# The exponent test of a float64-to-float32 conversion on ScalarE instead of VectorE, and the last small expert slot's first layer one step earlier

## The chip, the core and the metric

One core of one Trainium2 chip runs the whole program as one launch. The metric is the device time in microseconds, the median over several executions. TensorE is called PE here, VectorE DVE, ScalarE ACT, GpSimd POOL, and SP is the engine whose queue issues most of the DMAs.

## What is computed

Three stages follow one another on activations of 4 x 544 x 512: attention with a window and 32 global tokens, a mixture of eight experts with sticky routing, and a gated feed-forward block with a short convolution. Cut to what matters:

```python
x = attention(q_l, k_l, v_l, q_g, k_g, v_g)          # (4, 544, 512)
# experts: a token keeps the expert of the one before it, or takes a fresh one
h = np.maximum(x[b, s] @ w1[e], 0.0)                  # w1: 8 x 512 x 1024
out[b, s] = p[e] * (h @ w2[e])                        # w2: 8 x 1024 x 512
# feed-forward block; w_in, conv_w and w_out come as float64
h = np.maximum(x @ w_in, 0.0)                         # 512 x 1024
gate = 1.0 / (1.0 + np.exp(-conv3(h, conv_w)))
y = (h * gate) @ w_out                                # 1024 x 512
```

## The kernel before

Attention and routing fill the first 174 us. The expert stage then runs 20 slots, numbered 2 to 21, of up to 128 tokens of one expert each. With these inputs an expert takes one to four slots, and where its first slot holds few tokens (32 or less) that slot is "small": it multiplies the raw float32 weights with 32 token columns (`few_l1`, L1394, and `few_l2`, L1410). The other slots use weights split into a high part `wh` (a cast on ACT, L1045) and a low part `wl` (a subtraction on DVE, L1046), three matmuls for each product (L1110 for the first layer, L1126 for the second). Slots 2, 9, 13, 16 and 21 are small.

`step(s)` writes one slot's program: first layer of slot s, fetch of later weights, gather and transposition of slot s+1 (`turn_x`), the split of the first layer's weights if slot s+1 changes the expert (`resplit(s+1, 1)`, under an `If` at L1331), second layer of slot s-1 with its scatter to `y_dram` (L1083, on POOL), transposition of the hidden values of slot s (`turn_h`), the split of the second layer's weights (`resplit(s, 2)`). Each engine runs its own instructions in the order in which this is written. Since an `If` may write `wl`, PE's first layer waits until DVE has come past that `If`, taken or not.

Beside it, 16 chunks of `w_in` and `w_out` are turned from float64 into float32, one in each of the steps 3 to 18 (`convert`, `conv64`). The raw chunk lies in `fx`, `hi` and `lo` being the two 32-bit halves of each number. Six DVE instructions (L1012 to L1017) put the sign, exponent and fraction together and test the exponent, POOL adds the rounding bit (L1018), and one more DVE instruction, kept as a function in `self.conv`, flips a bit and masks tiny numbers to zero. It is called in the next step, right behind `turn_x` (`while self.conv`), and appears as L1019. The conversion stands ahead of the second layer where the next slot keeps its expert, and at the step's end where it doesn't.

The last slot, 21, is written by `last`, and the step of slot 20 is an ordinary `step`. In `last`, ACT and DVE also split the converted `w_in` into the registers of the first layer's weights (`split`), ACT loads the table for the sigmoid (L1234), and `load0` (L1501, called at the end of step 20's second layer) reads the first 544 rows of `y_dram` back for the feed-forward block; `scale0` (L1509) and `xt0` (L1516 to L1519) scale and transpose them. Each scatter waits for the one before it to land, `load0` waits for the scatter of slot 19, the scatter of slot 20 waits for `load0`, and the block's own first loads (L1535) wait for the scatter of slot 21. The block's units (L1585 first layer, L1609 and L1602 on ACT, L1604 and L1620 on DVE) then run to the end with its second layer (L1662).

Of the kernel before, what the change touches and what calls it, by code (L numbers as in the profile page):

```python
# [17 lines left out]
P = 128  # L18
# [985 lines left out]
DVE_F = (1, 3, 5, 7)  # L1004
POOL_K = {1: (), 2: ()}


def conv64(nc, raw, out):
    hi, lo = raw[:, :, 1], raw[:, :, 0]
    v = nc.vector  # L1010
    a = out.bitcast(I32)
    v.tensor_scalar(a, hi, 3, 0x7FFFFFFF, ALU.logical_shift_left, ALU.bitwise_and)  # L1012
    v.scalar_tensor_tensor(a, hi, -2 ** 31, a, ALU.bitwise_and, ALU.bitwise_or)
    v.tensor_scalar(hi, hi, 1, 21, ALU.logical_shift_left, ALU.logical_shift_right)
    v.tensor_scalar(hi, hi, 897.0, -1.0, ALU.is_ge, ALU.mult)
    v.scalar_tensor_tensor(a, lo, 29, a, ALU.logical_shift_right, ALU.bitwise_or)
    v.tensor_scalar(lo, lo, 28, 1, ALU.logical_shift_right, ALU.bitwise_and)  # L1017
    nc.gpsimd.tensor_tensor(a, a, lo, ALU.add)  # L1018
    return lambda: v.scalar_tensor_tensor(a, a, 0x40000000, hi, ALU.bitwise_xor, ALU.bitwise_and)  # L1019

# [32 lines left out]
class Moe:  # L1053
    def __init__(self, sig, tc, W, ident, x_dram, y_dram, rt, w1, w2, wi, wo):
# [3 lines left out]
        self.sig = sig  # L1058
        self.xs, self.xt, self.ht, self.hs, self.next, self.chg, self.sm = {}, {}, {}, {}, {}, {}, {}
        self.conv, self.raw = [], {}  # L1060

# [125 lines left out]
    def run(self, cw6, cwr, cw, f2):  # L1187
        nc, W, tc = self.nc, self.W, self.tc
        n = NSLOT - 3
        self.f2 = f2  # L1190
        for s in range(NA, n - 1):
            self.step(s)
            if s == NA + 17:
                self.conv.append(conv64(nc, cw6, cwr))
        self.last(n - 1, cwr, cw)
# [12 lines left out]
    def last(self, s, cwr, cw):  # L1208
        nc, W, f2 = self.nc, self.W, self.f2
        x, xs, hp = self.xt.pop(s), self.xs.pop(s), self.h_tile()  # L1210
# [4 lines left out]
        def split(a, b):  # L1215
            for k in range(a, b):
                W.split_k(1, W.f, k, nc.gpsimd if k in POOL_K[1] else nc.vector)

        def resplit(a, b):
            with self.tc.If(self.chg[s] != 0):  # L1220
                for k in range(a, b):
                    W.split_k(2, W.s, k, nc.gpsimd if k in POOL_L else nc.vector)

        def few1():
            self.few_l1(xs, hp, hs)
            split(0, NKC)

# [4 lines left out]

        self.either(s, few1, full1)
        nc.scalar.activation(self.sig, self.sig, AF.Sigmoid)  # L1234
        self.layer2(s - 1)
        self.fetch(s - 1, 2)
        self.conv_w(cwr, cw)
        self.rt.late_flag(s + 1, self.px.tile([P, 4, P], F32, tag="tr", name="lf")[0:1, 0, 0:1])
        for i in range(5):
            f2.scale0(i, self.ps)  # L1240
        resplit(0, 4)
        for i in range(2):
            f2.xt0(i, self.px)
        t = [self.ps.tile([P, 4, P], F32, tag="tr", name="hlp") for _ in range(2)]
        yp = self.y_tile()

        def few2():
            self.few_turn(hs, t[0])
            self.few_l2(hs, yp, y)

# [192 lines left out]
    def step(self, s):  # L1443
# [6 lines left out]
        self.turn_x(s + 1)  # L1450
        while self.conv:
            self.conv.pop()()
        if s < NA + 16:
# [284 lines left out]
def moe_kernel(ctx, tc, q_l, k_l, v_l, q_g, k_g, v_g, w_gate, w_local, w1, w2, w_in, conv_w, w_out, out):  # L1738
    nc = tc.nc
    outf = out.rearrange("b s d -> (b s) d")  # L1740
    with tc.manual_schedule():
# [38 lines left out]
        def hook(n, end):  # L1780
# [119 lines left out]
```

## Time and profile before

| what | us |
|---|---|
| median of 3 runs (lowest, highest) | 621.88 (618.85, 623.83) |
| the profiled execution: its own time | 619.98 |
| span from its first to its last instruction | 618.2 |
| PE busy in the span | 571.3 |

Times in the rows further down count from the start of the span. A row of the timeline gives an instruction's (or a run of equal instructions') start, its length, engine, line, operation, output and inputs, count, and in brackets how long the engine stood idle just before and what ended that. Rows of the windows give the busy time of each engine in a stretch, then the granted TensorE clock as a share of 2.4 GHz, the share of DMA time and GB/s.

### The profile page before, as it was taken

The page shows a single profiled execution, that of the slowest core. Times are in us where ns is not written, and L with a number is a line of the kernel's source. Part 1 is how long each engine was busy: PE and PEld are TensorE (multiplying, and loading weights), DVE is VectorE, ACT ScalarE, POOL GpSimd, SP SyncE. Part 2 cuts the span into 40 slices and gives each one's busy share as a digit, 9 for nine tenths or more (in the row PEclk, how much of TensorE's full clock was granted, in tenths as well). Part 3 has the DMA queues.
Part 4 walks back from the last instruction along what each step waited for, and adds up shares of the span by engine and source line. Part 5 has one row for each costly group of instructions (what it writes and reads, how often), then busy time and mean ns, then how long its engine had stood idle before and what let it go on. Part 6 is the DMA issues. An engine that isn't in the chain of part 4 may idle for free. (4 is left out here: it accounts for less than half of the span.)

```text
span 618.2 us, 16382 instructions
## 1 busy us (share of the span) xinstructions
PE 571.3 (92%) x6108; PEld 477.8 (77%) x6108; DVE 407.5 (66%) x854; ACT 308.3 (50%) x623; POOL 173.7 (28%) x226
## 2 busy tenths in 40 slices
PE   7779899888889999989989799979899999999997
PEld 6567677666667888768767688769898998998986
DVE  7868576875974867885687885366864484383330
ACT  5755555565225544652454724547753564463441
POOL 7655830034022423143132431010302313300100
PEclk9998899999999999999999989979899999999999
DMA  9989949568229765576357593322110201000001
GB/s 230 216 184 247 237 114 209 175 216 255 83 64 323 285 228 218 160 282 236 135 177 264 187 319 107 125 83 64 52 36 25 77 18 35 35 0 35 36 35 51
DMA packets 60643, 90.57 MB, mean 147 GB/s; under 512 B 25726, under 2 KB 34198, under 8 KB 60504
## 3 DMA queue, kind: packets, MB, share of 16 engines
q1 hardware_dynamic: 57016, 78.93, 42.1%
q0 software_dynamic: 3520, 10.23, 4.9%
q8 instruction: 65, 1.06, 0.7%
q14 instruction: 42, 0.34, 0.2%
HBM read 125.87 MB, written 15.79 MB: 229 GB/s over the span
## 5 line engine op out<-in xcount | busy, mean ns | idle before, releaser
L1604 DVE SCALAR_TENSOR_TENSOR fc<-f_hp,cw,fc 128x544 f32<-128x544 f32 (+2 forms) x66 | 51.7, 783 | 73.3 <-ACT fc L1602 71.9
L1046 DVE TENSOR_TENSOR wl<-ws,wh 128x512 fp32r<-128x512 f32 (+1 forms) x80 | 64.6, 869 | 8.1 <-ACT wh L1045 6.9
L1045 ACT CAST wh<-ws 128x512 fp32r<-128x512 f32 (+1 forms) x84 | 58.0, 770 | 1.7 <-DMA ws<-in_moe_w_dram 0.7
L1126 PE MATMUL yp<-wh,gh 128*128 128x512 f32 x136 | 54.8, 403 | 0.9 <-ACTq L1331 0.9
L1662 PE MATMUL f<-wh,fh 128*128 128x512 f32 (+1 forms) x144 | 54.8, 381 | 0.0
L1126 PE MATMUL yp<-wl,gh 128*128 128x512 f32 x136 | 53.5, 394 | 1.1 <-DVEq L1331 0.7
L1662 PE MATMUL f<-wh,fl 128*128 128x512 f32 (+1 forms) x144 | 54.4, 378 | 0.0
L1662 PE MATMUL f<-wl,fh 128*128 128x512 f32 (+1 forms) x144 | 54.4, 378 | 0.0
L1126 PE MATMUL yp<-wh,gl 128*128 128x512 f32 x136 | 53.3, 392 | 0.0
L1110 PE MATMUL hp<-wl,xh 128*128 128x512 f32 x136 | 45.5, 407 | 8.4 <-DVEq L1331 5.3
L1083 POOL DMA_INDIRECT y_dram<-ys,sidx x22 | 25.4, 1156 | 86.5 <-ACT ys L1438 38.7
L1309 ACT ACTIVATE hs<-hp 128x512 f32<-128x512 f32 x34 | 18.7, 594 | 61.3 <-PE hp L1110 61.3
L278 ACT ACTIVATE pr<-sp,nm 128x128 f32<-128x128 f32 x128 | 36.6, 376 | 24.7 <-DVE nm L275 24.7
L1110 PE MATMUL hp<-wh,xh 128*128 128x512 f32 x136 | 46.2, 412 | 0.2 <-ACT ys L1413 0.2
L1071 POOL DMA_INDIRECT xs<-x_dram,gidx x22 | 26.9, 1223 | 65.3 <-DMA ws<-in_moe_w_dram 34.0
L1110 PE MATMUL hp<-wh,xl 128*128 128x512 f32 x136 | 44.7, 401 | 0.0
L1018 POOL TENSOR_TENSOR wf<-wf,fx 128x512 int32<-128x512 int32 x16 | 20.9, 1304 | 74.0 <-DVE fx L1017 65.6
L1110 PEld LDWEIGHTS hp<-wl,xh 128*128 128x128 f32 x136 | 25.8, 193 | 15.8 <-DVEq L1331 6.6
L1609 ACT ACTIVATE f_hp<-f 128x544 f32<-128x544 f32 x31 | 19.4, 625 | 37.4 <-PE f L1585 33.4
L1103 DVE TENSOR_TENSOR gl<-hlp,gh 128x512 fp32r<-128x512 f32 x34 | 22.0, 685 | 18.3 <-ACT gh L1425 13.9
L1438 ACT COPY ys<-yp 128x512 f32<-128x512 f32 x15 | 8.9, 591 | 50.0 <-PE yp L1126 47.2
L1671 ACT COPY fy<-f 128x512 f32<-128x512 f32 (+1 forms) x18 | 10.1, 564 | 46.7 <-PE f L1662 46.7
(381 smaller groups left out, 1529.0 us busy)
## 6 DMA issues: line engine op xcount, KB each, us to landing
ws<-in_moe_w_dram SPq DMA_DIRECT2D x42, 2048.0 KB
fx<-y_dram SPq DMA_DIRECT2D x17, 256.0 KB
raw<-in_k_l_dram SPq DMA_DIRECT2D x16, 256.0 KB
x_dram<-x SPq DMA_DIRECT2D x16, 256.0 KB
fx<-in_moe_w_in_dram SPq DMA_DIRECT2D x8, 512.0 KB
fx<-in_moe_w_out_dram SPq DMA_DIRECT2D x8, 512.0 KB
out_dram<-fy SPq DMA_DIRECT2D x16, 256.0 KB
VA<-in_v_l_dram SPq DMA_DIRECT2D x20, 192.0 KB
```

The source lines that it names most:

```text
L278: nc.scalar.activation(pr[:, hp, :], sp[:, hp, :], AF.Exp, bias=nm[:, hp:hp + 1], scale=-1.0)
L1018: nc.gpsimd.tensor_tensor(a, a, lo, ALU.add)
L1045: (cp.tensor_copy if cp else self.nc.scalar.copy)(h, src[n][:, k, :])
L1046: eng.tensor_tensor(l, src[n][:, k, :], h.bitcast(F32), ALU.subtract)
L1071: self.nc.gpsimd.indirect_dma_start(out=xs, out_offset=None, in_=self.x_dram[0:n, :], in_offset=bass.IndirectOffsetOnAxis(ap=self.rt.gidx[ ...
L1083: self.nc.gpsimd.indirect_dma_start(out=self.y_dram[:, :], out_offset=bass.IndirectOffsetOnAxis(ap=self.rt.sidx[:, s:s + 1], axis=0), in_= ...
L1103: self.nc.vector.tensor_tensor(hl[1][:, a:a + 4], t, hl[0][:, a:a + 4].bitcast(F32), ALU.subtract)
L1110: self.nc.tensor.matmul(hp[c], a[:, k, :], b[:, 512 * c:512 * c + 512], start=k == 0 and m == 0, stop=k == NKC - 1 and m == 2)
L1126: self.nc.tensor.matmul(yp, a[:, k, :], b, start=k == 0 and m == 0, stop=k == NFC - 1 and m == 2)
L1604: nc.vector.scalar_tensor_tensor(c[:, a:b], hp[:, a + t:b + t], self.cw[:, t, f:f + 1], c[:, a:b], ALU.mult, ALU.add)
L1609: self.nc.scalar.activation(hp[:, 1:S + 1].rearrange("p (a c) -> p a c", a=2), p[:, :, 0:272], AF.Relu)
L1662: self.nc.tensor.matmul(yp[:, cs], x[:, c], w[:, cs], start=f == 0 and n == 0, stop=f == NFC - 1 and n == 2)
```

## The change

The test of the exponent moves to ACT: `Abs` of the upper half, read as float32, into a buffer `m`, then `Sign` of a limit less that, written as an integer, which is -1 (all bits) or 1. DVE then masks with one `tensor_tensor` ahead of POOL's addition; the constants are chosen so that no bit has to be flipped. The deferred instruction and `self.conv` go. `m` is the fifth input buffer of the feed-forward block, one for all conversions; `lim` is a column that was padding. In `last`, which now also writes slot 20's step, the split of `w_in` and the sigmoid's table come ahead of slot 19's second layer, slot 21's small first layer comes ahead of `turn_h` of slot 20 and so ahead of its second layer, its transposition takes a buffer of its own, and its scatter comes ahead of the last three `xt0`. The diff, without the passing on of `lim` and its `memset`:

```diff
@@ conv64
+TINY = (9 - 2.0 ** -20) * 2.0 ** -18
-def conv64(nc, raw, out):
+def conv64(nc, raw, out, m, lim):
     hi, lo = raw[:, :, 1], raw[:, :, 0]
-    v = nc.vector
-    a = out.bitcast(I32)
-    v.tensor_scalar(a, hi, 3, 0x7FFFFFFF, ALU.logical_shift_left, ALU.bitwise_and)
-    v.scalar_tensor_tensor(a, hi, -2 ** 31, a, ALU.bitwise_and, ALU.bitwise_or)
-    v.tensor_scalar(hi, hi, 1, 21, ALU.logical_shift_left, ALU.logical_shift_right)
-    v.tensor_scalar(hi, hi, 897.0, -1.0, ALU.is_ge, ALU.mult)
+    v, a, n = nc.vector, out.bitcast(I32), m.shape[0]
+    nc.scalar.activation(m, hi.bitcast(F32), AF.Abs)
+    nc.scalar.activation(m.bitcast(I32), m, AF.Sign, bias=lim[0:n], scale=-1.0)
+    v.tensor_scalar(a, hi, 3, 0x3FFFFFFF, ALU.logical_shift_left, ALU.bitwise_and)
+    v.scalar_tensor_tensor(a, hi, -2 ** 30, a, ALU.bitwise_and, ALU.bitwise_or)
     v.scalar_tensor_tensor(a, lo, 29, a, ALU.logical_shift_right, ALU.bitwise_or)
     v.tensor_scalar(lo, lo, 28, 1, ALU.logical_shift_right, ALU.bitwise_and)
+    v.tensor_tensor(a, a, m.bitcast(I32), ALU.bitwise_and)
     nc.gpsimd.tensor_tensor(a, a, lo, ALU.add)
-    return lambda: v.scalar_tensor_tensor(a, a, 0x40000000, hi, ALU.bitwise_xor, ALU.bitwise_and)
...
@@ Moe.run
-        for s in range(NA, n - 1):
+        for s in range(NA, n - 2):
             self.step(s)
...
@@ Moe.last
-        nc, W, f2 = self.nc, self.W, self.f2
+        nc, W, f2, p = self.nc, self.W, self.f2, s - 1
+        self.small(s)
+        self.layer1(p)
+        self.fetch(p, 1)
+        self.turn_x(s)
+        self.resplit(s, 1)
...
-        def few1():
+        r = nc.values_load(self.rt.esi[0:1, 5, s:s + 1], min_val=0, max_val=1,
+                           engines=[mybir.EngineType.Activation, mybir.EngineType.DVE])
+        with self.tc.If(r != 0):
+            split(0, NKC)
+        nc.scalar.activation(self.sig, self.sig, AF.Sigmoid)
+        self.layer2(p - 1)
+        self.fetch(p - 1, 2)
+        f2.load0()
+        with self.tc.If(self.sm[s] != 0):
             self.few_l1(xs, hp, hs)
-            split(0, NKC)
+        self.turn_h(p)
+        self.resplit(p, 2)
...
-        self.either(s, few1, full1)
-        nc.scalar.activation(self.sig, self.sig, AF.Sigmoid)
-        self.layer2(s - 1)
-        self.fetch(s - 1, 2)
+        tq = self.px.tile([P, 4, P], F32, tag="tr", name="hlq")
+        self.either(s, lambda: self.few_turn(hs, tq), full1)
         self.conv_w(cwr, cw)
...
+        self.layer2(p)
+        self.fetch(p, 2)
...
-        self.either(s, few2, full2)
+        self.either(s, lambda: self.few_l2(hs, yp, y), full2)
         resplit(4, NFC)
...
+        self.scatter(s, y)
         for i in range(2, 5):
-            f2.xt0(i, self.px)
-        self.scatter(s, y)
+            f2.xt0(i, self.ps if i == 4 else self.px)
@@ Moe.step
-        while self.conv:
-            self.conv.pop()()
...
-        if s == hi - 2:
-            self.f2.load0()
```

On DVE, the conversion of one chunk (`wf` is the converted weight, `fx` the raw chunk). Before:

```order
L1012 TENSOR_SCALAR wf_3966<-fx 128x512
L1013 SCALAR_TENSOR_TENSOR wf_3966<-fx,wf_3966 128x512
L1014 TENSOR_SCALAR fx<-fx 128x512
L1015 TENSOR_SCALAR fx<-fx 128x512
L1016 SCALAR_TENSOR_TENSOR wf_3966<-fx,wf_3966 128x512
L1017 TENSOR_SCALAR fx<-fx 128x512
```

and now, where `fx` is also the mask:

```order
L1014 TENSOR_SCALAR wf_3967<-fx 128x512
L1015 SCALAR_TENSOR_TENSOR wf_3967<-fx,wf_3967 128x512
L1016 SCALAR_TENSOR_TENSOR wf_3967<-fx,wf_3967 128x512
L1017 TENSOR_SCALAR fx<-fx 128x512
L1018 TENSOR_TENSOR wf_3967<-wf_3967,fx 128x512
```

Two of the four fast single-input instructions are gone, and a `TENSOR_TENSOR` has come.

On DVE, the stretch from `turn_x` of the next slot (`xl`) to the `If` that PE's next first layer waits for. Before:

```order
L1340 COMPARE_AND_BRANCH
L1340 UNCONDITIONAL_BRANCH
L1103 TENSOR_TENSOR xl<-xlp,xh 128x512
L1340 UNCONDITIONAL_BRANCH
L1019 SCALAR_TENSOR_TENSOR wf_3966<-wf_3966,fx 128x512
L1324 TENSOR_LOAD esi
L1331 COMPARE_AND_BRANCH
```

and now:

```order
L1349 COMPARE_AND_BRANCH
L1349 UNCONDITIONAL_BRANCH
L1103 TENSOR_TENSOR xl<-xlp,xh 128x512
L1349 UNCONDITIONAL_BRANCH
L1333 TENSOR_LOAD esi
L1340 COMPARE_AND_BRANCH
```

The instruction L1019 that stood ahead of the flag's `TENSOR_LOAD` and the `If` (L1331, now L1340) is gone.

On ACT, the last slots: `ys_3454` is the output buffer of slot 20 in the build before, `wf_3966` the converted `w_in`. Before:

```order
L1045 CAST wh_2_2729<-wf_3966 128x1024
L1045 CAST wh_3_2731<-wf_3966 128x1024
L1340 UNCONDITIONAL_BRANCH
L1045 CAST wh_0_2725<-wf_3966 128x1024
L1045 CAST wh_1_2727<-wf_3966 128x1024
L1340 UNCONDITIONAL_BRANCH
L1234 ACT_TABLE_LOAD
L1234 ACTIVATE warm<-warm 128x1
L1340 COMPARE_AND_BRANCH
L1413 COPY ys_3454<-yp 32x128 x4
L1340 UNCONDITIONAL_BRANCH
L1438 COPY ys_3454<-yp 128x512
```

and now, where `ys_3456` is the buffer of slot 19:

```order
L1045 CAST wh_0_2726<-wf_3967 128x1024
L1045 CAST wh_1_2728<-wf_3967 128x1024
L1045 CAST wh_2_2730<-wf_3967 128x1024
L1045 CAST wh_3_2732<-wf_3967 128x1024
L1231 UNCONDITIONAL_BRANCH x2
L1233 ACT_TABLE_LOAD
L1233 ACTIVATE warm<-warm 128x1
L1349 COMPARE_AND_BRANCH
L1422 COPY ys_3456<-yp 32x128 x4
L1349 UNCONDITIONAL_BRANCH
L1447 COPY ys_3456<-yp 128x512
L1349 UNCONDITIONAL_BRANCH
```

The four casts and the table load stood behind slot 21's small first layer and ahead of slot 20's output; they now stand ahead of slot 19's.

## Rows read from the trace of the kernel before

**Rows 1.** Page, part 1, and one group of part 5 (busy, mean ns; idle).

```profile
PE 571.3 (92%) x6108; PEld 477.8 (77%) x6108; DVE 407.5 (66%) x854; ACT 308.3 (50%) x623; POOL 173.7 (28%) x226
...
L1018 POOL TENSOR_TENSOR wf<-wf,fx 128x512 int32<-128x512 int32 x16 | 20.9, 1304 | 74.0 <-DVE fx L1017 65.6
```

**Rows 2.** Timeline, PE: first layers of slots 11, 15 and 18.

```profile
276.81 0.55 PE L1110 MATMUL hp<-wl,xh 128*128 128x512 f32 x1 [2.12 <-DVEq L1331]
...
322.55 0.73 PE L1110 MATMUL hp<-wl,xh 128*128 128x512 f32 x2 [2.10 <-DVEq L1331]
...
355.45 1.09 PE L1110 MATMUL hp<-wl,xh 128*128 128x512 f32 x2 [3.14 <-DVE wl L1046]
```

**Rows 3.** Windows: PE, PEld, DVE, ACT, POOL busy (x), clock, DMA.

```profile
276.80:283.70 6.90, 6.89 (x24) 5.51 (x25) 4.29 (x8) 0.15 (x1) 2.33 (x2) 0.75 0.84 260
322.50:328.00 5.50, 5.45 (x25) 4.51 (x26) 4.30 (x8) 0.30 (x1) 1.94 (x2) 1.00 0.74 235
355.40:362.40 7.00, 6.95 (x25) 5.55 (x26) 5.98 (x8) 0.46 (x2) 0.88 (x1) 0.76 0.92 301
...
411.00:416.50 5.50, 5.50 (x23) 5.20 (x24) 5.07 (x10) 2.18 (x4) 0.93 (x7) 0.50 0.20 47
```

**Rows 4.** Timeline, DVE, slots 9 to 11.

```profile
259.47 0.43 DVE L1012 TENSOR_SCALAR wf<-fx 128x512 int32<-128x512 int32 x1 [0.33 <-DVEq L1331]
259.93 0.69 DVE L1013 SCALAR_TENSOR_TENSOR wf<-fx,wf 128x512 int32<-128x512 int32 x1
...
264.04 0.69 DVE L1019 SCALAR_TENSOR_TENSOR wf<-wf,fx 128x512 int32<-128x512 int32 x1
...
268.85 5.61 DVE L1046 TENSOR_TENSOR wl<-ws,wh 128x512 fp32r<-128x512 f32 x8 [0.56 <-PE hp L1110]
...
276.01 0.68 DVE L1019 SCALAR_TENSOR_TENSOR wf<-wf,fx 128x512 int32<-128x512 int32 x1
```

**Rows 5.** Timeline, ACT, slots 8 and 9.

```profile
264.84 0.59 ACT L1438 COPY ys<-yp 128x512 f32<-128x512 f32 x1 [5.03 <-PE yp L1126]
...
266.25 4.27 ACT L1045 CAST wh<-ws 128x512 fp32r<-128x512 f32 x8 [0.55 <-DMA ws<-in_moe_w_dram]
```

**Rows 6.** Timeline, ACT, slot 12 and the last slots.

```profile
297.39 3.90 ACT L1045 CAST wh<-ws 128x1024 fp32r<-128x1024 f32 x4 [0.31 <-ACT xs L1360]
...
387.75 0.27 ACT L1360 COPY xs<-xlp 128x128 f32<-128x128 f32 x1
392.92 0.59 ACT L1438 COPY ys<-yp 128x512 f32<-128x512 f32 x1 [4.89 <-PE yp L1126]
...
395.99 3.88 ACT L1045 CAST wh<-wf 128x1024 fp32r<-128x1024 f32 x4
399.89 1.28 ACT L1234 ACT_TABLE_LOAD   x1
```

**Rows 7.** Timeline, POOL: scatters of slots 19, 20 and 21.

```profile
393.79 0.99 POOL L1083 DMA_INDIRECT y_dram<-ys,sidx  x1 [8.59 <-ACT ys L1438]
405.88 0.97 POOL L1083 DMA_INDIRECT y_dram<-ys,sidx  x1 [11.10 <-issue]
410.68 0.97 POOL L1083 DMA_INDIRECT y_dram<-ys,sidx  x1 [3.83 <-ACT f_x0h L1518]
```

**Rows 8.** DMA issues from 404 to 406.5 us: the scatter of slot 20.

```profile
y_dram<-ys,sidx POOLq DMA_INDIRECT x1, 4.0
```

**Rows 9.** Timeline, SP: `load0`, and the block's first load.

```profile
398.68 1.29 SPq L1501 DMA_DIRECT2D fx<-y_dram  x3
...
413.70 0.68 SPq L1535 DMA_DIRECT2D fx<-y_dram  x1
```

**Rows 10.** Waits of SP from 380 to 440 us: total, times, longest.

```profile
SPq L1535 <- DMA y_dram<-ys,sidx: 8.9, 1, 8.9
```

**Rows 11.** Timeline, ACT and PE, in the feed-forward block.

```profile
421.51 0.73 ACT L1541 ACTIVATE fx<-fx,gate 128x512 f32<-128x512 f32 x1 [2.90 <-DMA fx<-y_dram]
...
439.78 0.44 PE L1550 MATMUL f_tr<-ident,fx 128*128 128x128 f32 x2 [2.82 <-DVE fxl L1552]
```

More of the change, by code (lines that the diff above doesn't have):

```diff
@@ L1053, with __init__ @@
 class Moe:
-    def __init__(self, sig, tc, W, ident, x_dram, y_dram, rt, w1, w2, wi, wo):
+    def __init__(self, sig, lim, tc, W, ident, x_dram, y_dram, rt, w1, w2, wi, wo):
         self.nc, self.tc = tc.nc, tc
@@ L1057, in __init__ @@
         self.rt, self.w1, self.w2, self.wi, self.wo = rt, w1, w2, wi, wo
-        self.sig = sig
+        self.sig, self.lim = sig, lim
         self.xs, self.xt, self.ht, self.hs, self.next, self.chg, self.sm = {}, {}, {}, {}, {}, {}, {}
-        self.conv, self.raw = [], {}
+        self.raw = {}
     def open(self, ctx):
@@ L1190, in run @@
         self.f2 = f2
-        for s in range(NA, n - 1):
+        for s in range(NA, n - 2):
             self.step(s)
             if s == NA + 17:
-                self.conv.append(conv64(nc, cw6, cwr))
+                conv64(nc, cw6, cwr, f2.x_in[4][0:3 * NFC, 0:P], self.lim)
         self.last(n - 1, cwr, cw)
@@ L1216, in split @@
             for k in range(a, b):
-                W.split_k(1, W.f, k, nc.gpsimd if k in POOL_K[1] else nc.vector)
+                W.split_k(1, W.f, k, nc.vector)
         def resplit(a, b):
@@ L1221, in resplit @@
                 for k in range(a, b):
-                    W.split_k(2, W.s, k, nc.gpsimd if k in POOL_L else nc.vector)
-        def few1():
+                    W.split_k(2, W.s, k, nc.vector)
+        r = nc.values_load(self.rt.esi[0:1, 5, s:s + 1], min_val=0, max_val=1,
[7 more added lines that the diff above has]
+        with self.tc.If(self.sm[s] != 0):
             self.few_l1(xs, hp, hs)
-            split(0, NKC)
+        self.turn_h(p)
+        self.resplit(p, 2)
+        t = [self.ps.tile([P, 4, P], F32, tag="tr", name="hlp") for _ in range(2)]
         def full1():
@@ L1243, in last @@
             f2.xt0(i, self.px)
-        t = [self.ps.tile([P, 4, P], F32, tag="tr", name="hlp") for _ in range(2)]
         yp = self.y_tile()
-        def few2():
-            self.few_turn(hs, t[0])
-            self.few_l2(hs, yp, y)
         def full2():
@@ L1469, in step @@
         if NA < s <= NA + 16:
-            self.conv.pop()
             with self.tc.If(self.chg[s + 1] != 0):
@@ L1484, in convert @@
         n, k, o = self.chunk(s)
-        self.conv.append(conv64(self.nc, self.raw[s], self.W.f[n][:, k, o:o + 512]))
+        conv64(self.nc, self.raw[s], self.W.f[n][:, k, o:o + 512], self.f2.x_in[4], self.lim)
 class Ffn2:
@@ L1753, in moe_kernel @@
         L = cp.tile([P, NT, 9], F32, name="L")
-        cp.tile([P, PAD_C], F32, name="pad_c")
+        lim = cp.tile([P, PAD_C], F32, name="pad_c")[:, 0:1]
+        nc.vector.memset(lim, TINY)
         cc = Consts()
@@ L1796, in hook @@
                 W = Weights(nc, hl, st)
-                m = todo["m"] = Moe(warm, tc, W, ident, x_dram, y_dram, rt, w1, w2, w_in.bitcast(I32),
+                m = todo["m"] = Moe(warm, lim, tc, W, ident, x_dram, y_dram, rt, w1, w2, w_in.bitcast(I32),
                                     w_out.bitcast(I32))
```

## The prediction

> **What bounds the kernel now.** I read the page first: PE is busy for 571.3 of 618.2 us [rows 1], so only what keeps PE waiting, or slows its clock, can change the time much. The timeline of PE comes next. From 200 us to the end of slot 20 it has no idle time worth a word outside three places, all three in the first layer of the second slot behind a small one: slots 11, 15 and 18 wait 2.12, 2.10 and 3.14 us [rows 2]. The reader is to see what is waited for. At the first two it is the sequencer of DVE at L1331, the `If` that DVE must have come past; at the third it is `wl` itself, which DVE writes behind the same `If`.
>
> The windows say that two of the places cost more than the wait. Behind the 2.12 and the 3.14 us the granted clock is 0.75 and 0.76 over the next layer, which is part of the time at 1.2 instead of 2.4 GHz; behind the 2.10 us it is 1.00, and the same 24 matmuls and their neighbours take 5.45 instead of 6.89 and 6.95 us of PE's time [rows 3]. So a place costs its wait, and in two of three cases another 1.4 or 1.5 us.
>
> Why DVE is late is in its own timeline [rows 4]: between 259.47 and 276.7 us it runs two conversions, the eight `wl` of the small slot's second layer (5.61 us) and two L1019, hardly with a gap. The `If` follows the second L1019 within 0.1 us of PE's start at 276.81. The other two places have the same sequence.
>
> The last part is bound by something else. In the feed-forward block ACT waits 2.90 us for the first rows of its next batch, and from there the chain of waits runs over ACT and DVE to 439.78, where PE, after 2.82 us of idle time, takes over to the end [rows 11]. Those rows are loaded at the end of a row of DMAs: scatter of slot 19 at 393.79, `load0` at 398.68, scatter of slot 20 at 405.88, of slot 21 at 410.68, the block's loads at 413.70 [rows 7, 9]; SP's longest wait for its data names a scatter [rows 10].
>
> **Part 1, the conversion.** On DVE a conversion loses two `TENSOR_SCALAR` of 0.43 us and the L1019 of 0.69, and gains one `TENSOR_TENSOR`. No row has that on integers; the nearest has two inputs in SBUF and 512 columns, `wl`, at 5.61/8 = 0.70 us. The bounds are 0.43, as for one input, and 1.30, what POOL's L1018 takes for the same form [rows 1]. I take 0.70: 2 x 0.43 + 0.69 - 0.70 = 0.85 us less for each conversion. At each of the three places two conversions and two L1019 lie in the way, so DVE comes past the `If` 1.7 us earlier (0.5 to 2.2 by the bounds). What is late next: PE wants its first `wl` 2.1, 2.1 and 3.1 us before DVE is there, so waits of about 0.4, 0.4 and 1.4 us stay. 3 x 1.7 = 5.1 us.
>
> With waits of 0.4 and 1.4 us I expect the clock not to fall, since 2.10 us left it at 1.00 [rows 3]: 6.89 - 5.45 + 6.95 - 5.45 = 2.9 us. The other end is 0, if it falls all the same. The Trainium skill ("TensorE: Matmul & The Clock Gate", section "What's actually happening") says that the monitor behind the clock runs freely and doesn't start with the kernel, so that the point of a change varies. The rows agree so far as 2.12 us brought the lower level and 2.10 us didn't; it is why I give the fall a chance of its own below.
>
> In the other thirteen or so conversions PE doesn't wait for DVE, and 0.85 us less there is worth nothing.
>
> ACT gains two instructions for each conversion. An ACT instruction of 512 columns takes 4.27/8 = 0.53 us [rows 5]; no row reads every second word, so between 0.5 and 1.1. I take 0.6 each, 1.2 for the pair. It stands behind `turn_x` and ahead of slot s-1's output, where ACT waits 5.03 us for PE [rows 5]: that wait is the cover. Two waits are new. DVE's mask waits for `Sign`; DVE needs about 0.43 + 0.69 + 0.69 + 0.43 = 2.2 us for what stands ahead of it, ACT 1.2. And `Abs` waits for the mask of the former chunk, since there is one `m`. In the step of slot 9 that mask ends at about 259.47 + 2.9 = 262.4; ACT, which has nothing to do from 259.81 (264.84 - 5.03), is held to there, and its pair ends by 263.6, ahead of the output at 264.84. In the step after it, `Abs` waits until the eight `wl` are done (now 274.46, then about 1 us earlier), and behind it queue the output of slot 9 and the `gh` casts of slot 10, which PE needs only at the second layer of slot 10, some 6 us later. I cost both at nothing. If the cover is gone, each us by which the pair is late is a us at each of the three places.
>
> A rule speaks against the move. The Trainium skill ("ScalarE: Activation LUTs", section "Rules for kernel authors") wants cheap elementwise work on VectorE, and budgets about 0.3 us and 0.83 ns for each element: an estimate of 0.72 us an instruction, 1.45 the pair. The trace has 0.53, and the wait of 5.03 us covers either; but it is true that ACT's two are dearer than the two DVE instructions they replace.
>
> **Part 2, the last slots.** The four casts of `w_in` and the table load now stand ahead of slot 19's output. ACT is free at 387.75 + 0.27 = 388.0; two flags and branches at 0.31 each (what lies ahead of the casts at 297.39 [rows 6]) bring the casts to 388.6, their 3.88 us to 392.5, the table's 1.28 to 393.8, the small sigmoid to 394.0. Slot 19's output was at 392.92 [rows 6], so it comes 1.1 us later, and with it its scatter and `load0`: 399.8 instead of 398.7. PE's second layer of slot 20 also moves back, by slot 21's first layer and its transposition, some 1.2 us; but the scatter of slot 20 waits for `load0` (405.88, long behind its own output), so it comes at 407.0. It lands 4.0 us later [rows 8], at 411.0. Before, it landed at 409.9, and the scatter of slot 21 then still waited for a cast of the last `xt0` until 410.68 [rows 7]; now it stands ahead of those in the program and goes at 411.1. So the block's loads are 0.4 us later, and so are the 421.51 and the 439.78. PE comes to the block about 1 us earlier than its 410.94, and has nothing from it, since the chain over ACT and DVE ends last. Sum of the part: +0.4 us. Bounds: -0.8, if ACT's casts start so early that slot 19's output isn't delayed; +2, if slot 21's scatter still finds 0.7 us to wait and PE, idle behind the block's third unit, drops its clock.
>
> **The sum.** -5.1 - 2.9 + 0.4 = -7.6 us, against the profiled execution's own 619.98: 612.4. That execution lies 1.9 us below the median of 621.88; I take the difference to the median, 614.3. The ratio is 0.988.
>
> **Rivals.** (a) The clock falls to its lower level at slot 11 or 18 all the same: one of the two costs 1.4 or 1.5 us, 615.8, both 617.2. For it: at slot 18 1.4 us stay, and PE's work just before, matmuls on 32 token columns, is light. Against it: 2.10 us at slot 15, behind the same light work, did nothing.
>
> (b) The end loses more: the bound of +2 instead of +0.4, 615.9. For it: three DMAs in a row, of which the first starts later. Against it: the one wait that goes.
>
> (c) The change doesn't shorten the wait: `Sign` is late by the 0.85 us that the conversion saves, because ACT is held by `m`, or the `TENSOR_TENSOR` costs POOL's 1.30. Then part 1 gives 0 to 1.5 us (3 x 2 x (0.43 + 0.43 + 0.69 - 1.30)) and the clock falls as before: 620.8 to 622.3, say 621.5. Against it: the times of `Sign` and mask worked out above leave 1 us and more.
>
> (d) Slower: the clock in the feed-forward block. PE comes to the block 1 us earlier, but its fourth unit needs a buffer that ACT frees only behind the 421.51, so PE stands idle ahead of it for some 1.5 us (410 + 5.7 + 2 x 2.9 = 421.5, against 421.9, the scaling's 0.73 and one more ACT instruction), where it ran through before. If the clock falls there and PE stays at 1.2 GHz to the end of the chain, a unit takes as long as at 411 us, where the clock is 0.50: 5.5 us for 23 matmuls [rows 3]. The chain gives each of its five units (439.78 - 421.51)/5 = 3.7 us, so 5 x 1.8 = 9 us come on top: 623.3. It decides from two units on at the lower level, when the 2.82 us of slack are used up. Against it: units in a row brought the clock back by 416.5 in the kernel before.
>
> **How the numbers follow.** Forecast (both clocks kept, end +0.4) 0.57; (a) 0.19; (b) 0.10; (c) 0.09; (d) 0.05. About 1% is what a measurement of this kernel can tell from no change, so faster by over 1% means below 615.7. The forecast is there nearly always (0.54 of its 0.57), (a) and (b) in about a third (0.06 and 0.04): 0.64. Slower by over 1% needs (d) with the clock at slots 11 and 18 as it was: 0.03. The rest, 0.33, is within 1%. The range for 8 of 10: down to 610.5, where the mask costs 0.43 and the end its -0.8 and the median's own scatter helps by 1; up to 619.0, which takes in (a) and (b) with the like scatter; (c), (d) and what lies below are left out.
>
> **What would show it.** In the profile after, PE's waits in the first layers of slots 11, 15 and 18 should be about 0.4, 0.4 and 1.4 us, the clock over those layers 1.00, the mask 0.65 to 0.75 us on DVE, `Abs` and `Sign` 0.5 to 0.7 us each and never waited for by DVE. Slot 19's output should follow the table load by 0.3 us, its scatter come 5 us ahead of `load0`, and slot 21's scatter 4 us behind slot 20's. PE's idle time at the end of the chain should be longer than 2.82 us. I am wrong if the waits at slots 11 and 15 stay above 1 us, or if the time from PE's last first layer of the experts to the end grows by more than 2 us.

## The result, and the profile after

The changed kernel takes 611.35 us, median of 4 runs (609.61 to 612.43), beside 621.36 us for the kernel before (618.85 to 623.83, 4 runs): a ratio of 0.9847, 95% interval 0.9804 to 0.9890. That is 10.0 us less, where 7.6 were forecast, and 611.35 lies in the range. The profiled execution took 610.53 us, its span 608.6 us instead of 618.2. Here and below, times are medians, while the ratios are estimated from the undisturbed runs alone, so that a ratio can differ a little from that of the two medians.

Line numbers have moved: L1331 is now L1340, `xl` and `gl` stay at L1103, a conversion is L1012 and L1013 (`Abs` and `Sign` on ACT) and L1014 to L1018 (DVE, L1018 the mask).

First the page's part 1, to set beside [rows 1].

```profile
PE 570.2 (94%) x6108; PEld 477.5 (78%) x6108; DVE 395.0 (65%) x821; ACT 331.4 (54%) x657; POOL 171.7 (28%) x226
```

DVE has 12.5 us less to do and ACT 23.1 more. What that is worth is seen on PE in the first layers of slots 11, 15 and 18 (timeline: start, us, instruction, idle time ahead of it in brackets), where [rows 2] has 2.12, 2.10 and 3.14 us:

```profile
275.51 0.70 PE L1110 MATMUL hp<-wh,xh 128*128 128x512 f32 x2 [0.24 <-PE hlp L1433]
276.05 0.65 PE L1110 MATMUL hp<-wl,xh 128*128 128x512 f32 x2
...
318.51 0.72 PE L1110 MATMUL hp<-wl,xh 128*128 128x512 f32 x2
...
349.41 0.73 PE L1110 MATMUL hp<-wl,xh 128*128 128x512 f32 x2 [0.67 <-DVE wl L1046]
```

At slots 11 and 15 the first matmul on `wl` doesn't wait any more, at slot 18 it waits 0.67 us. The windows over these layers (us, then busy time of PE, PEld, DVE, ACT and POOL, the granted clock, DMA) have the clock at 1.00 three times, against 0.75, 1.00 and 0.76 in [rows 3]:

```profile
272.00:280.00 8.00, 7.76 (x94) 6.35 (x93) 6.48 (x12) 5.18 (x12) 1.96 (x2) 1.00 0.90 280
316.00:322.00 6.00, 5.79 (x45) 4.35 (x40) 4.47 (x9) 3.51 (x8) 0.09 (x1) 1.00 0.80 242
349.40:356.40 7.00, 6.99 (x33) 5.77 (x34) 5.88 (x8) 5.58 (x12) 1.01 (x1) 1.00 0.99 335
390.70:398.20 7.50, 7.44 (x26) 5.71 (x27) 2.45 (x6) 0.00 (x0) 0.00 (x0) 0.77 0.49 153
```

The fourth row is new: in slot 20's second layer the clock now falls. DVE's timeline at the first place answers to [rows 4]:

```profile
260.75 0.43 DVE L1014 TENSOR_SCALAR wf<-fx 128x512 int32<-128x512 int32 x1 [0.43 <-DVEq L1340]
...
263.01 0.68 DVE L1018 TENSOR_TENSOR wf<-wf,fx 128x512 int32<-128x512 int32 x1
263.73 0.69 DVE L1103 TENSOR_TENSOR xl<-xlp,xh 128x512 fp32r<-128x512 f32 x1
265.05 0.43 DVE L1014 TENSOR_SCALAR wf<-fx 128x512 int32<-128x512 int32 x1 [0.63 <-DVEq L1340]
...
268.58 5.64 DVE L1046 TENSOR_TENSOR wl<-ws,wh 128x512 fp32r<-128x512 f32 x8 [0.52 <-PE hp L1110]
```

From the start of the place's first conversion to the eight `wl` it is 7.83 us instead of 9.38, and no L1019 follows the second `xl`. Two things have gone: the instructions that I counted, and the idle time ahead of the first `xl`, 0.04 us here (263.73 - 263.01 - 0.68). In the trace of before it was 0.63 us, put down to "issue", that is, to nothing that the profile shows:

```profile
262.19 0.43 DVE L1017 TENSOR_SCALAR fx<-fx 128x512 int32<-128x512 int32 x1
263.25 0.69 DVE L1103 TENSOR_TENSOR xl<-xlp,xh 128x512 fp32r<-128x512 f32 x1 [0.63 <-issue]
```

On ACT, beside [rows 5]:

```profile
259.12 0.72 ACT L1012 ACTIVATE fx<-fx 128x512 f32<-128x512 f32 x1 [0.27 <-ACTq L1340]
259.87 0.72 ACT L1013 ACTIVATE fx<-fx,pad_c 128x512 int32<-128x512 f32 x1
...
263.78 0.68 ACT L1012 ACTIVATE fx<-fx 128x512 f32<-128x512 f32 x1 [2.26 <-DVE wf L1018]
264.50 0.73 ACT L1013 ACTIVATE fx<-fx,pad_c 128x512 int32<-128x512 f32 x1
266.07 0.59 ACT L1447 COPY ys<-yp 128x512 f32<-128x512 f32 x1 [0.85 <-PE yp L1126]
```

`Abs` is held 2.26 us by the mask of the former chunk, the pair ends at 265.2, and the output of slot 8 still waits 0.85 us for PE: the cover was 5.03 us, 0.85 are left, and that output was not late.

At the end, ACT from 381 us (against [rows 6]), the scatters of slots 19, 20 and 21 on POOL ([rows 7]), `load0` and the block's loads on SP ([rows 9]), and PE ahead of slot 20's second layer:

```profile
381.51 3.90 ACT L1045 CAST wh<-wf 128x1024 fp32r<-128x1024 f32 x4 [1.16 <-DMA y_dram<-ys,sidx]
385.43 1.28 ACT L1233 ACT_TABLE_LOAD   x1
...
386.83 0.57 ACT L1447 COPY ys<-yp 128x512 f32<-128x512 f32 x1
```

```profile
387.68 0.99 POOL L1083 DMA_INDIRECT y_dram<-ys,sidx  x1 [10.28 <-ACT hs L1405]
399.08 0.98 POOL L1083 DMA_INDIRECT y_dram<-ys,sidx  x1 [10.41 <-ACTq L1225]
403.12 0.97 POOL L1083 DMA_INDIRECT y_dram<-ys,sidx  x1 [3.06 <-ACTq L1277]
```

```profile
390.50 3.54 SPq L1505 DMA_DIRECT2D fx<-y_dram  x5
...
406.02 2.79 SPq L1539 DMA_DIRECT2D fx<-y_dram  x5
```

```profile
390.38 0.16 PE L962 MATMUL lf<-c_ones,late 128*1 128x1 bf16 x1 [1.88 <-DVE esi L963]
```

Slot 19's scatter is followed by `load0` after 2.8 us (4.9 before), and slot 21's follows slot 20's after 4.0 (4.8 before). The 1.88 us are a wait that I had not seen: the flag of late tokens (`lf`, a 1x1 matmul) waits for a small instruction on DVE (the row names `esi`, L963), DVE comes to it only behind `gl` of slot 20, and PE's second layer of slot 20 is queued behind `lf`.

Where the 9.6 us of the span went: up to slot 9's first layer the profile after is 1.3 us longer; from there to the start of slot 21's first layer it has 127.15 us instead of 136.97; from there to the end 223.45 instead of 224.56. The middle stretch, called the stretch below, is the measure of the conversion. In the new order slot 21's layer starts 0.8 us earlier, so 136.97 is to be read as 136.1 there (136.11 and 136.09 in e2 and e2b).

### The profile page after: what moved, and what is told of

It reads as the page before. It is cut to its first block, busy times and chain, and to the rows that moved or that the text cites. A ratio compares the mean times of both kernels' runs of the same rounds, so it can differ in the third digit from the quotient of the medians.

```text
span 608.6 us, 16465 instructions
## 1 busy us (share of the span) xinstructions
PE 570.2 (94%) x6108; PEld 477.5 (78%) x6108; DVE 395.0 (65%) x821; ACT 331.4 (54%) x657; POOL 171.7 (28%) x226
## 5 line engine op out<-in xcount | busy, mean ns | idle before, releaser
L1126 PE MATMUL yp<-wl,gh 128*128 128x512 f32 x136 | 54.8, 403 | 0.4 <-DVEq L1340 0.4
L1110 PE MATMUL hp<-wl,xh 128*128 128x512 f32 x136 | 43.9, 394 | 2.1 <-DVEq L1340 1.1
L1071 POOL DMA_INDIRECT xs<-x_dram,gidx x22 | 25.6, 1163 | 70.2 <-ACT pr L278 34.0
L1019 POOL TENSOR_TENSOR wf<-wf,fx 128x512 int32<-128x512 int32 x16 | 20.9, 1308 | 60.0 <-DVE wf L1018 54.7
L1126 PEld LDWEIGHTS yp<-wh,gh 128*128 128x128 f32 x136 | 26.3, 193 | 8.4 <-issue 2.3
L1666 PEld LDWEIGHTS f<-wh,fl 128*128 128x128 f32 x144 | 27.1, 188 | 5.1
```

The source lines that it names most:

```text
L1071: self.nc.gpsimd.indirect_dma_start(out=xs, out_offset=None, in_=self.x_dram[0:n, :], in_offset=bass.IndirectOffsetOnAxis(ap=self.rt.gidx[ ...
L1110: self.nc.tensor.matmul(hp[c], a[:, k, :], b[:, 512 * c:512 * c + 512], start=k == 0 and m == 0, stop=k == NKC - 1 and m == 2)
L1126: self.nc.tensor.matmul(yp, a[:, k, :], b, start=k == 0 and m == 0, stop=k == NFC - 1 and m == 2)
L1666: self.nc.tensor.matmul(yp[:, cs], x[:, c], w[:, cs], start=f == 0 and n == 0, stop=f == NFC - 1 and n == 2)
```

## The experiments

Each ratio is to runs of the kernel before on the same chip, with its 95% interval; the kernel before took 617.5 to 619.9 us there.

**One part alone.** e1 has the new `conv64` with `run` and `last` of before, and `load0` back in `step`; e2 and e2b have the new `last` with the old `conv64` and its deferred instruction.

e1, against the changed kernel (and `last` as before):

```diff
-        for s in range(NA, n - 2):
+        for s in range(NA, n - 1):
...
+        if s == hi - 2:
+            self.f2.load0()
```

e2 and e2b, against the changed kernel (and `conv64` as before, its mask called behind `turn_x`):

```diff
-        conv64(self.nc, self.raw[s], self.W.f[n][:, k, o:o + 512], self.f2.x_in[4], self.lim)
+        self.conv.append(conv64(self.nc, self.raw[s], self.W.f[n][:, k, o:o + 512]))
```

> The new conversion with the last slots in their old order. Theory: nearly the whole gain is DVE's shorter way to the If at slots 11, 15 and 18. PE's waits there are 0, 0 and about 0.7 us as in the changed kernel, the clock over these layers stays at 1.00, and the way from the start of the small slot's first layer to the end of the x transposition after the next-but-one first layer is 23 to 24 us at each place (before 26.9, 25.0, 27.6). From the start of slot 19's second layer to the end of the span it takes 231 us as before. Time 8 to 9 us below before, about 612.5 to 613.5. Rival: the new order of the last slots is what brought the part that my forecast lacked (about 2 us): then 231 us shrinks only in the next kernel and this one stays at 6 to 7 us below before, about 615.

e1 took 608.05 us, 0.9832 (0.9797 to 0.9868), 10.5 us less than before where 8 to 9 were expected. PE's waits are 0, 0.30 and 1.10 us, the clock is 1.00 behind each, and the stretch is 127.99 us in the old order. Within the intervals the conversion alone is the whole gain, which is the first theory.

> The old conversion with the last slots in their new order. Theory of my forecast: waits at slots 11, 15 and 18 stay at 2.1, 2.1 and 3.1 us with the low clock at two of them; the end costs 0.4 us, 231.5 us from the start of slot 19's second layer on; time 621.8, no difference from before. Rival 1, from the two traces: the end gains 1 to 2 us (229 to 230 us), because slot 20's scatter no longer stands behind load0's five transfers and PE's clock falls less in the feed-forward block; time 619.5 to 620.5. Rival 2: the order at the end is worth 3 us or more; below 618.5.

e2 took 618.31 us, 0.9992 (0.9962 to 1.0022), with waits of 2.01, 2.01 and 3.04 us. But from the start of slot 19's second layer its profile needs 228.44 us to the end of the span (called its end below) instead of 231.09. The time shows no gain and the profile shows one, so e2 ran again:

> The old conversion with the last slots in their new order, as in e2, to narrow its interval (0.9962 to 1.0022) and to see a second profile. If the new order is worth the 2.7 us by which the first profile was shorter between slot 19's second layer and the block's first fxl (50.0 instead of 52.7), the ratio is about 0.995 or 0.996; if my forecast of +0.4 us holds, 1.000 to 1.001. The stretch itself should be 50 to 50.8 us again, unless it hangs on how long slot 19's scatter takes to land.

e2b took 620.59 us, 0.9998 (0.9972 to 1.0025), and its end 228.45 us. The contradiction is the same, so the suspect is the profile of before.

> The kernel before, unaltered, profiled a second time. Open is why the kernels with the old conversion and the new last slots take as long as before, though both of their profiles are 2.7 us shorter (228.4 us) from slot 19's second layer to the end of the span than the profile of before (231.1). If 231.1 us is what this end usually takes, it is 230.5 to 231.5 again, and what the last slots gain is lost ahead of slot 9, where the profiles scatter by several us anyway. If the profile of before was a long one, it is 229 to 230 us. The waits at slots 11, 15 and 18 are 2.1, 2.1 and 3.1 us and the clock low behind the first and the third in either case.

c0 took 618.59 us, 1.0002 (0.9965 to 1.0039), and its end 228.39 us, shorter than either expectation. So the profile that the prediction was worked from had a long end: scatter to scatter and load to load its DMAs landed later. On POOL and SP in c0:

```profile
392.99 0.99 POOL L1083 DMA_INDIRECT y_dram<-ys,sidx  x1 [8.59 <-ACT ys L1438]
404.20 0.97 POOL L1083 DMA_INDIRECT y_dram<-ys,sidx  x1 [10.21 <-ACT hs L1402]
408.02 0.97 POOL L1083 DMA_INDIRECT y_dram<-ys,sidx  x1 [2.85 <-ACT f_x0h L1518]
```

```profile
397.37 2.24 SPq L1501 DMA_DIRECT2D fx<-y_dram  x5
...
410.76 2.81 SPq L1535 DMA_DIRECT2D fx<-y_dram  x5
```

From slot 19's scatter to the block's loads it is 17.8 us (410.76 - 392.99), where [rows 7, 9] have 19.9 and the changed kernel 18.3. The clock was another difference: in the block's first 5.5 us it was 0.50 in [rows 3] and is 1.00 in c0:

```profile
410.20:415.70 5.50, 5.32 (x40) 5.11 (x41) 5.05 (x10) 3.57 (x6) 0.28 (x6) 1.00 0.50 132
```

It is unlikely to have made the end long, since PE stands idle at the chain's end all the same (2.82 us before, 2.56 in c0).

Single profiles can't price the order of the last slots. The old order has an end of 231.09 (before), 228.39 (c0) and 230.16 us (e1), the new one 228.44 and 228.45 (e2, e2b), 229.11 (the profile after) and 228.38 (c1, below). The ratios can: e2, e2b, and e1 against c1 show no gain and no loss, within 0.3% at best, some 1.8 us.

**What about the conversion.** e3 puts the test back on DVE (seven DVE instructions, mask not deferred), e9 carries out the mask twice, e13 adds an AND of one element.

e3:

```diff
-    nc.scalar.activation(m, hi.bitcast(F32), AF.Abs)
-    nc.scalar.activation(m.bitcast(I32), m, AF.Sign, bias=lim[0:n], scale=-1.0)
...
-    v.tensor_tensor(a, a, m.bitcast(I32), ALU.bitwise_and)
+    v.tensor_scalar(hi, hi, 1, 21, ALU.logical_shift_left, ALU.logical_shift_right)
+    v.tensor_scalar(hi, hi, 897.0, -1.0, ALU.is_ge, ALU.mult)
+    v.tensor_tensor(a, a, hi, ALU.bitwise_and)
```

e9, and e13:

```diff
+    v.tensor_tensor(a, a, m.bitcast(I32), ALU.bitwise_and)
```

```diff
+    v.tensor_tensor(a[0:1, 0:1], a[0:1, 0:1], m[0:1, 0:1].bitcast(I32), ALU.bitwise_and)
```

> The changed kernel, with the exponent test (two tensor_scalar) back on DVE, but the mask still ahead of POOL's addition, so nothing is deferred to the next step. DVE's busy time for a conversion is 0.43 + 0.69 + 0.69 + 3 x 0.43 + 0.68, about 3.8 us, as much as before with its deferred instruction (3.1 + 0.69). Theory (busy time of DVE is what counts): 0.86 us come back for each conversion, 1.7 at each place; waits of about 1.3, 1.1 and 2.4 us at slots 11, 15 and 18, the low clock at slot 18 at least, time 616 to 620. Rival (what counted is the deferred instruction with the gap ahead of xl and the wait for POOL, not the move to ACT): waits below 0.5 us, time as the changed kernel's, 611 to 613.

e3 took 619.13 us, 0.9994 (0.9964 to 1.0025); the gain is gone. The stretch is 136.90 us, the waits on PE are those of before or longer:

```profile
275.46 0.50 PE L1110 MATMUL hp<-wl,xh 128*128 128x512 f32 x1 [2.20 <-DVEq L1340]
321.50 0.50 PE L1110 MATMUL hp<-wl,xh 128*128 128x512 f32 x1 [2.18 <-DVEq L1340]
354.75 0.75 PE L1110 MATMUL hp<-wl,xh 128*128 128x512 f32 x1 [3.40 <-DVE wl L1046]
```

That the mask isn't deferred gives nothing by itself; the rival falls. But the waits exceed the 1.3, 1.1 and 2.4 us of the theory by about 1 us each.

> The changed kernel with the mask (the AND on DVE, 0.68 us) carried out twice in each conversion. Theory: each microsecond of DVE work ahead of the If comes back as a wait at slots 11, 15 and 18: 2 x 0.72 = 1.4 us at each, so waits of about 1.4, 1.6 and 2.1 to 2.5 us; the clock stays at 1.00 at slot 15, and at slots 11 and 18 it shows whether less than 2 us bring it down. Time 4.5 us above the changed kernel, and up to 3 us more if the clock falls at both. Rival: the gap that came back ahead of xl with the test on DVE is a matter of how many instructions DVE has in a conversion and not of their time; then the waits are 1.0 or less.

e9 took 617.14 us, 0.9988 (0.9962 to 1.0013). That is 9.2 us above the changed kernel on the same chip (c1, below), where 4.5 to 7.5 were expected. The waits are 1.91, 1.83 and 2.74 us, the stretch 133.80 us, and the clock is low at slot 18 alone (0.74; 1.00 at slots 11 and 15). Again the waits grow by more than the 1.4 us of the theory at each place. In the trace the idle time ahead of the first `xl` is back, 0.66 us.

> The changed kernel with one more DVE instruction in each conversion, an AND of a single element behind the mask: six instructions as before, but hardly more busy time (about 0.1 us). Open is the gap ahead of xl behind a place's first conversion: 0.63 to 0.66 us where a conversion has six DVE instructions, 0.37 with seven, 0.04 with five. Theory (it hangs on the number of instructions, not on their time): the gap is 0.4 us or more again, the way from the first conversion's start to the eight wl is 8.4 us or more instead of 8.0, and the waits at slots 11, 15 and 18 grow by 0.5 us or more. Rival (it hangs on when the engine comes to it): the gap stays below 0.2 us, the waits grow by 0.3 us at most. Time within 2 us of the changed kernel in either case.

e13 took 614.42 us, 0.9926 (0.9885 to 0.9966). DVE at the first place, and PE:

```profile
258.65 0.69 DVE L1018 TENSOR_TENSOR wf<-wf,fx 128x512 int32<-128x512 int32 x1
259.37 0.15 DVE L1019 TENSOR_TENSOR wf<-wf,fx 1x1 int32<-1x1 int32 x1
260.73 0.69 DVE L1104 TENSOR_TENSOR xl<-xlp,xh 128x512 fp32r<-128x512 f32 x1 [1.21 <-ACT fx L1012]
```

```profile
272.99 0.50 PE L1111 MATMUL hp<-wl,xh 128*128 128x512 f32 x1 [1.42 <-DVEq L1341]
316.49 0.50 PE L1111 MATMUL hp<-wl,xh 128*128 128x512 f32 x1 [1.19 <-DVEq L1341]
348.48 0.50 PE L1111 MATMUL hp<-wl,xh 128*128 128x512 f32 x1 [2.20 <-DVE wl L1047]
```

Against c1, the changed kernel run again (below), an instruction of 0.15 us costs 1.0 to 1.4 us of waiting at each place, and the clock at slot 18 (0.74 instead of 1.00); the stretch is 132.21 us, 5.1 more than without it. The count of instructions matters, as the theory had it; the time was to stay within 2 us of the changed kernel's, and that part is missed. The trace names `Abs` on ACT as the releaser; but in the profile after `xl` starts at 263.73, ahead of the `Abs` at 263.78 that follows the mask, so it doesn't wait for that. What the traces have in common is another distance: `xl` starts 1.0 to 1.4 us behind the start of the conversion's last instruction wherever six or seven stand in it, be that one 0.15, 0.43 or 0.69 us long (c0, e3, e9 and e13, five places each), and right behind it (0.64 to 0.73 us, about its own duration) where five do. A sixth place, at about 240 us, doesn't count: there `xl` waits for the cast `xh` on ACT, with five instructions too (2.2 us). Between the two DVE has only branches and a register load to get past. With five instructions it seems to have them behind it while the five still run. What sets the limit between five and six no run shows. The Trainium skill ("Advanced Engine Details and Errata", section "Engine Queue Depths") gives VectorE a queue of 8. That figure alone doesn't explain these rows, where the distance jumps between five and six (0.72 us in the profile after and 1.36 in e13, at the first place).

**Is the work on ACT hidden?** e11 carries out `Abs` three times.

```diff
+    nc.scalar.activation(m, m, AF.Abs)
+    nc.scalar.activation(m, m, AF.Abs)
```

> The changed kernel with Abs carried out three times in each conversion, 1.4 us more on ACT each time, so that ACT's share of a conversion is 2.9 us instead of 1.4. Theory (the ACT pair is hidden): in the timeline of the changed kernel Sign ends 2.4 us ahead of the mask at the first conversion of a place and 1.7 us ahead at the second, so DVE never waits for ACT; the output that queues behind comes 0.6 us later, and PE doesn't wait for it. Waits at slots 11, 15 and 18 stay at 0, 0.2 and 1.0 us, time as the changed kernel's, 0.983 to 0.988 of before. Rival (the cover is thin): DVE's mask, or the eight casts of the small slot's second layer on ACT, come later by up to 1.4 us, and waits of about 1 us come back at the three places, 0.990 or more.

e11 took 609.44 us, 0.9820 (0.9789 to 0.9850), with waits of 0, 0 and 0.71 us and a stretch of 126.81 us. Twice the work on ACT is hidden too: `Abs` is held 0.95 us by the former mask instead of 2.26, and the cover pays for the rest.

```profile
265.41 0.68 ACT L1012 ACTIVATE fx<-fx 128x512 f32<-128x512 f32 x1 [0.95 <-DVE wf L1020]
```

**The last slots.** c1 is the changed kernel again. e5 moves the table load behind slot 21's first transposition; e4 moves the flag `lf` behind slot 20's second layer and the scaling; e8 has the table load of e5 and the flag behind slot 21's output.

The table load (e5, e8):

```diff
-        nc.scalar.activation(self.sig, self.sig, AF.Sigmoid)
         self.layer2(p - 1)
...
         self.either(s, lambda: self.few_turn(hs, tq), full1)
+        nc.scalar.activation(self.sig, self.sig, AF.Sigmoid)
```

The flag, as e8 has it (in e4 its new place is behind the five `scale0`):

```diff
-        self.rt.late_flag(s + 1, self.px.tile([P, 4, P], F32, tag="tr", name="lf")[0:1, 0, 0:1])
         self.layer2(p)
...
         self.scatter(s, y)
+        self.rt.late_flag(s + 1, self.px.tile([P, 4, P], F32, tag="tr", name="lf")[0:1, 0, 0:1])
```

> The changed kernel, with the flag of late tokens (a 1x1 matmul on PE and two small DVE instructions) behind slot 20's second layer and behind the scaling, so that PE's second layer of slot 20 no longer stands behind a wait for DVE. Theory: the new wait of 1.88 us goes (0.2 to 0.7 us for gl stay), the clock doesn't fall, the layer takes 5.8 us instead of 7.4, and slot 20's output comes 2.5 to 3.4 us earlier; its scatter then waits only for load0's reads, about 397.2 instead of 399.1, and all behind it, to the end, comes about 1.9 us earlier: 1 to 2 us below the changed kernel. Rival: the chain at the end hangs on the landing of load0 and on the block's ACT and DVE work, so the time stays within 0.5 us of the changed kernel.

e4 took 613.32 us, 0.9920 (0.9887 to 0.9952), dearer than c1's 0.9844. The 1.88 us go (0.39 us for ACT and 0.34 for DVE stay) and the clock holds, but `load0` comes 12.7 us behind the start of slot 19's second layer instead of 11.0, slot 20's scatter at 19.8 as in the changed kernel (19.6), and a new wait stands ahead of the second transposition, since its buffer follows the flag's:

```profile
396.97 0.48 PE L1520 MATMUL f_tr<-ident,fx 128*128 128x128 f32 x1 [3.48 <-DVE esi L964]
```

What was gained in one place went in another, and more; of the two expectations neither holds.

> The changed kernel itself, unaltered, beside the next three on the same chip. If the clock's fall in slot 20's second layer (7.37 us there in the profile after, 5.73 to 5.78 in the kernels with the last slots in the new order and another conversion, or the reverse) hangs on the changed kernel's own order of waits, the layer takes 7.4 us again; if it is chance, 5.7. Ratio to before 0.983 to 0.988 in either case.

c1 took 607.98 us, 0.9844 (0.9798 to 0.9890). Slot 20's second layer takes 7.36 us (7.37 in the profile after, 7.39 in e11), though e2, e2b, e3, e5 and e9 have the same wait of 1.87 to 1.90 us and 5.74 to 5.78. It repeats in the two profiles of the changed kernel, and what tells the kernels apart is open. The waits are 0, 0.23 and 1.00 us, the end 228.38 us long.

> The changed kernel with the sigmoid and its table load (1.28 + 0.2 us on ACT) moved from ahead of slot 19's output to behind slot 21's first transposition, where ACT is idle for 8 us. Theory: slot 19's output, its scatter and load0 come about 1.4 us earlier, load0's data too, but slot 20's scatter then waits for its own output (18.7 us behind the start of slot 19's second layer, or 17.1 where the clock holds), so the end gains 0 to 0.5 us: no difference that can be measured from the changed kernel. Rival: the end hangs on load0 alone, 1.4 us less.

e5 took 607.09 us, 0.9829 (0.9785 to 0.9873), as c1. Slot 19's scatter comes 1.5 us earlier and `load0` only 0.6, the end is 227.35 us long.

> The table load behind as in the kernel before this one, and the flag of late tokens (PE's 1x1 matmul and its two DVE instructions) moved behind slot 21's output, so that PE's second layer of slot 20 doesn't stand behind the 1.88 us wait and no f_tr stands behind the flag. Theory: both inputs of slot 20's scatter come earlier, load0's reads by 1.4 us and slot 20's output by 1.5 us (3 us where the clock had fallen); from slot 19's second layer to the block's first fxl 50 us or less instead of 52.1, and 1.5 to 2.5 us less than the changed kernel in all. Rival: the landing of slot 19's scatter (2.8 us in three kernels, 4.6 in one) decides and eats the gain.

e8 took 607.90 us, 0.9856 (0.9815 to 0.9897), as c1. The 1.88 us are gone, slot 20's output is 2.9 us earlier, its scatter 1.3, and the end is 228.39 us as in c1: PE waits 2.89 us for `fxl` instead of 1.12. No version of the end is measurably faster than the changed kernel. That the end hangs on the row of DMAs is not shown: in e8 the block's loads start 25.3 us behind slot 19's second layer and in c1 26.2, and the ends are equal.

## Why the prediction was right

**The conversion, -8.0 forecast, -8.9 measured.** Between the profiles of c0 and c1, from the start of the small slot's first layer to the transposition behind the third layer from there, the three places lose 3.74, 1.55 and 3.64 us (27.43, 25.51 and 28.22 become 23.69, 23.96 and 24.58). At the first place, in c0 and then in c1:

```profile
255.94 1.93 PE L1394 MATMUL hp<-ws,xs 128*32 128x256 f32 x32
...
276.05 1.08 PE L1110 MATMUL hp<-wl,xh 128*128 128x512 f32 x2 [2.13 <-DVEq L1331]
...
282.77 0.60 PE L1353 MATMUL xlp<-ident,xs 128*128 128x128 f32 x4
```

```profile
253.69 1.93 PE L1403 MATMUL hp<-ws,xs 128*32 128x256 f32 x32
...
276.78 0.60 PE L1362 MATMUL xlp<-ident,xs 128*128 128x128 f32 x4
```

The clock's part is the 22 matmuls behind the wait: 6.88 and 6.91 us become 5.3 twice, 3.2 in all where I had 2.9. The waits' part is the rest, 5.7, where I had 5.1. The term that was mis-sized is "1.7 us earlier" at each place: from c0 to c1 the waits fall by 2.1, 1.7 and 2.1 us (from 2.13, 1.97 and 3.11), and the first of these stops at 0. Its counted parts are right (the mask takes 0.68 us, forecast 0.70), but the idle time ahead of `xl` went as well. It stood in the trace of before, and I passed over it with "hardly with a gap". So 0, 0.2 and 1.0 us of waiting are left (0, 0 and 0.67 in the profile after), not 0.4, 0.4 and 1.4.

Of the 16 chunks six lie at the three places, so the others are ten, not "thirteen or so"; nothing in the sum hangs on that.

The reason was also narrower than I thought. I reckoned with busy time only; e3 and e9 agree with that in sign, but in e13 a sixth instruction costs about 1 us at a place, though it takes 0.15. By luck the change that I priced by time also goes from six to five.

**The clock kept.** It was, but not because 2.10 us had left it alone. At slot 15 no wait of 1.19 to 2.18 us brought it down (seven profiles); at slot 11 each of 2.00 to 2.20 us did (five) and 1.42 and 1.91 didn't; at slot 18 each of 2.20 to 3.40 did (seven) and up to 1.10 didn't. Where it fell, the clock was 0.74 to 0.76 over the layer behind the wait (part of it at 1.2 instead of 2.4 GHz), and elsewhere 1.00. At slots 11 and 15 of e3, behind waits of 2.20 and 2.18 us:

```profile
275.50:282.10 6.60, 6.60 (x22) 5.27 (x23) 4.98 (x9) 0.00 (x0) 2.15 (x2) 0.74 0.94 327
321.50:326.60 5.10, 5.10 (x22) 4.19 (x23) 4.56 (x9) 0.00 (x0) 0.78 (x1) 1.00 0.89 275
```

So a wait of the same length brings the clock down at one of these places and not at another, and that repeats from kernel to kernel; why is open. The Trainium skill ("TensorE: Matmul & The Clock Gate", section "What's actually happening") lets the point of a change vary from run to run. At these three places the rows show no such scatter, while at slot 20 the same 1.87 to 1.90 us brought the clock down in four kernels' profiles and not in five others'.

**ACT hidden.** Right: `Abs` and `Sign` take 0.67 to 0.73 us where I had 0.6, and the order of events was as I worked it out, `Abs` held, the pair done ahead of the output. The estimate of 0.72 us from the Trainium skill ("ScalarE: Activation LUTs", section "Rules for kernel authors") agrees with these rows better than my figure from the dense casts. Its preference for VectorE didn't bear on the time, since ACT had the room and DVE had not (e11).

**The end, +0.4 forecast, nothing measurable found** (e1 against c1, e2 and e2b against before; the intervals are 0.3% wide to either side at best, so the runs can't tell +0.4 us from 0). The steps were less good than the sum. Slot 19's output came 1.5 us later (7.34 instead of 5.81 us behind the start of its layer), as forecast in kind. But `load0` didn't follow it: its distance from the scatter shrank from 4.9 (4.4 in c0) to 2.8 us. I did not see the wait of 1.88 us at `lf`, nor the clock falling behind it. They cost nothing that can be measured, since e8, which has neither, takes as long. PE's idle time at the chain's end became 1.72 us, not longer than 2.82.

**The rivals.** (a) didn't come about at slots 11 and 18. (b) wants a loss of 2 us at the end, and (d) the low clock to the end of the chain: neither is there. The clock does fall at the start of the block, where it is 0.69 for 5.5 us in the profile after, but it is 1.00 from there on. Rival (c), the mask late by `Sign` or dear, is excluded by e11 and by the mask's 0.68 us.

The 10.0 us of the medians are 8.9 at the three places; the rest is within the interval of the ratio (1.96% to 1.10% less, 12.2 to 6.8 us).

## What to carry to other kernels

Where PE waits for an in-order engine to come past an `If`, list everything that engine does there, its idle gaps and the number of its instructions too, and not just busy time: here one instruction of 0.15 us cost 5 us, and going from seven of them (six and the deferred one) to five saved 9. Work moved to an engine with idle time is free only as long as what queues behind it isn't late, which a kernel with that work doubled shows in one run. Before a part is credited with what two single profiles differ by, profile the kernel before a second time: the end of this one differs by 2.7 us between two profiles of the same kernel.

## What the runs showed that I had not expected

- Five or six instructions in a conversion: `xl` 0.04 us or 0.3 to 1.2 us behind the last one's end.
- The clock falls by place: no wait of up to 2.18 us at slot 15 brought it down (seven profiles), while each of 2.00 to 2.20 us at slot 11 did (five).
- Slot 20's second layer is at the low clock for part of its time in after, c1 and e11 (7.36 to 7.39 us) and in e13 (7.08), and not in five others with the same wait of 1.87 to 1.90 us ahead of it (5.74 to 5.78).
- The same scatter of 128 x 512 is followed by the load that waits for it after 2.8 us (after, c1, e2, e2b, e3, e11), 3.2 (e9, e13), 3.8 (e5, e8) or 4.4 to 4.9 (before, c0, e1, e4).
